# A gated mix of a long convolution and a token-mixing MLP: row-wise first layer norm, x1 seeded into PSUM for the fourth product, mirrored frequency sets, and a new written-out order

## Chip, cores and metric

The kernel runs on one core of one Trainium2 chip. The metric is device time in microseconds (us). In the text PE is TensorE (PEld its weight loads), ACT is ScalarE, DVE is VectorE, POOL is GpSimd and SP is SyncE, which here only issues DMAs.

## What is computed

The input q (called x here) has 2048 tokens of 640 channels in bfloat16. The reference, cut to what matters:

```python
x = A_q
g = sigmoid((x * gate_w).sum(-1, keepdims=True))
# branch a: shift convolution over 4 taps, times v, then a causal convolution of length 2048 per channel
kv = shift_conv(k, shift_k) * v
a  = x * (irfft(rfft(pad(kv)) * rfft(pad(ssm_k)))[:2048] + kv * ssm_D)
# branch b: two MLP halves; the first shifts four channel groups by +1, -1, +2, -2 tokens
h  = gelu(layernorm(x) @ w1)
x1 = x + shift_groups(h) @ w2
b  = x1 + gelu(layernorm(x1) @ w3) @ w4
out = g * a + (1 - g) * b
```

## The kernel before

**Tiling.** A token is numbered 1024c + 8p + rho: p is the partition, and the 16 pairs (rho, c) are the token tiles, 128 tokens by 640 channels each. A "row" is one rho, so two tiles. Everything lies in one SBUF tensor (`arena`) and one PSUM tensor (`PS`), and the trace shows only these two names. PSUM is dealt out as four pairs of banks: each matmul job takes a pair, and gives it back when its evictions are done.

**Branch b.** LN1 takes mean and variance of x with `bn_stats` on DVE (L640, tag `bn`), the power -0.5 on POOL (L646, `ln`), and writes the normalised tile on ACT (L465, `xn`). PE transposes it (L620, `xTp`) and ACT evicts the transposes (L480, `xTe`). `mm1` (L715) multiplies by w1, with a gelu on eviction (`gelu1`). One fifth of each product, the tail (`gelu1t`), is moved between partitions by DMAs on POOL's queue (L743, `tail`). `mm2` (L760) multiplies by w2, ten matmuls of 320 columns per tile, and two matmuls with the identity (L762) add x. Its eviction makes x1 (`x1`). LN2 takes its sums on ACT for half of the rows (with an accumulator in the `x1` eviction, and a `Square` pass, `sq`) and with `bn_stats` on DVE for the other half. `xn` is again on ACT, and a DMA transpose (L615, `xT`) writes the operand of `mm3` (L792, gelu on eviction `gelu3`). `mm4` (L808) has 24 matmuls per tile and two more with the identity for x1 (L810). Its eviction `B` scales by 1 - g and overwrites x1 in place. w3 is loaded over w1 and w2, so its DMA (POOL's queue) waits for the last `mm2`.

**Branch a.** `kv` on DVE (L453, the line of every `tensor_tensor`) makes k_shift * v in four chunks of 128x2560, eight instructions each. The filter is transposed on PE (L578, `tap`) and evicted by ACT (L583). The convolution is a transform over 512 odd frequencies, for each of two halves of the channels (half 0, 1) and each of two frequency sets (kap 0, 1). That is four *units*, numbered 2*half + kap. `forward` (L844, `fwdh` for the filter, `fwdk` for kv) has 8 jobs of four 320-column matmuls per signal and unit, each evicted by ACT (L480, 128x640: `Sh`, `Sk`). On DVE a unit then runs `bh`, `win`, `bk` (butterflies and window), `pw` (the complex product) and `fold`, one after the other, on slots of 128x5120. `inverse` (L934, `inv`) has 8 rows of eight matmuls per half. ACT evicts them with the gate g (`gy`, 128x320), DVE multiplies by q and adds to the tile that `B` left (`fin`), and SP writes the output.

**What sets the order.** Nothing is ordered by hand in the body. `Prog.schedule` simulates all engines with assumed costs and lets ready instructions go by a table of ranks per tag and stage (`P.PRIO`). What comes out is a fixed list per engine, and each engine runs its list strictly in order. `assign_waits` puts a semaphore wait ahead of an instruction where another engine's result is needed.

In before, the fixed lists have these places that the prediction speaks of: PE runs 40 of the 256 `fwd` matmuls ahead of `mm2`, 88 between the `mm2` jobs and 36 behind the last of them; the rest comes between `mm3`, `mm4` and `inv`. DVE's 15 instructions from 54.53 us on are the last twelve of `kv` with three of `bh` of unit 0 among them; the last of `kv` is the last of the 15. The two 128x1280 instructions after DVE's 1.74 us wait for ACT, at 82.85 us, are `win` of unit 0, and its last `fold` (unit 3) ends the run of 102 instructions from 126.85 us on.

Of the kernel before, what the change touches and what calls it, by code (L numbers as in the profile page):

```python
# [1 line left out]

# [15 lines left out]
class Job:  # L18
    __slots__ = ("pair", "pe", "evicts")

    def __init__(self):
        self.pair = None
        self.pe = None
        self.evicts = []


class Node:
    __slots__ = ("idx", "eng", "fns", "deps", "users", "cost", "lat", "bytes", "kind", "job", "prio",
                 "start", "end", "base", "ordinal", "seq", "waits", "inc", "value", "sem", "final", "snap", "missing", "tag")

    def __init__(self, idx, eng, fns, cost, kind, tag):
# [8 lines left out]
        self.lat = 0.1  # L40
        self.bytes = 0
        self.job = None
        self.prio = 0.0
# [9 lines left out]
        self.missing = 0  # L53

# [24 lines left out]
class Prog:  # L79
    def __init__(self, nc):  # L80
        self.nc = nc
        self.nodes = []
        self.stage = ""
        self.writers = {}
        self.readers = {}
# [28 lines left out]

    def op(self, eng, fn, r=(), w=(), cost=0.2, job=None, group=None, tag=""):
        node = self._new(eng, [fn], cost, "c", r, w, group, tag)
        if job is not None:
            node.deps.add(job.pe)
            node.job = job
            job.evicts.append(node)  # L120
        return node

    def pe(self, fns, r=(), cols=0, tag=""):
        job = Job()
        cost = cols / 2400.0 + 0.004 * len(fns) + 0.02
        node = self._new("pe", fns, cost, "c", r, (), None, tag)
        node.job = job
        job.pe = node
        return job

    def dma(self, queue, fn, r=(), w=(), nbytes=0, cost=0.1, kind="dma", group=None, final=False, tag=""):
        node = self._new(queue, [fn], cost, kind, r, w, group, tag)
        node.bytes = nbytes
        node.final = final
        return node

    RATE = 390e3
    PRIO = {}

    def schedule(self):  # L140

        for n in self.nodes:
            n.base = frozenset(n.deps)
            for d in n.deps:
                d.users.append(n)
        for n in reversed(self.nodes):
            tail = max((u.prio for u in n.users), default=0.0)
            n.prio = tail + (n.cost if n.kind == "c" else n.cost + 2.0 + n.bytes / self.RATE)
        for n in self.nodes:
            n.prio = self.PRIO.get(n.tag, n.prio)  # L150
        self._forward()

    def _forward(self):
        nodes = self.nodes
        rate = self.RATE
        for n in nodes:
# [3 lines left out]
            if n.job is not None:  # L160
                n.job.pair = None
# [4 lines left out]
        pair_job = [None] * PAIRS  # L166
        link = 0.0
        xlink = 0.0

        def arrive(n):  # L170
            known_at[n] = max((d.end + (d.lat if d.eng != n.eng else 0.06) for d in n.deps), default=0.0)
            ready[n.eng].append(n)

        def open_pairs():
            return [(pair_free[i], i) for i in range(PAIRS)
                    if pair_job[i] is None or all(v.end is not None for v in pair_job[i].evicts)]
# [7 lines left out]
        while left:  # L184
            best = None
            pairs = open_pairs()
            for e in ENGS:
                if e == "pe" and not pairs:
                    continue
                for n in ready[e]:  # L190
                    t = max(known_at[n], free[e])
                    if e == "pe":
                        others = [d.end for ev in n.job.evicts for d in ev.deps if d is not n]
                        if any(x is None for x in others):
                            continue
                        t = max(t, min(pairs)[0], max(others, default=0.0) - n.cost)
# [12 lines left out]
            elif n.kind == "dma":  # L209
                link = max(link, t) + n.bytes / rate  # L210
                n.end = link + 2.0
            else:
                xlink = max(xlink, t + 1.0) + 1.2
                n.end = xlink + 1.5
            if e == "pe":
                pick = min(pairs)[1]
# [803 lines left out]
```

## Time and profile before

| what | value |
|---|---|
| runs of before | 254.81, 255.53 and 256.13 us (median 255.53) |
| span of the profiled execution, first to last instruction | 253.7 us |
| median less that span | 1.8 us |
| mean granted TensorE clock | 0.990 |
| DMA over the span | 27.81 MB, of which 20.55 MB on the hardware queue that SP issues to |
| DVE `tensor_tensor` (L453), all forms | 195.8 us busy in 208 instructions |

The profiled execution's own time is its span and a little around it. No separate figure is listed for it, so 1.8 us, the median less the span, stands for what lies around. A row of a timeline reads: start, duration, engine, line, operation, output and input, count, and in brackets the idle time ahead of it with what ended it. The chain of work that ended last is read back from the last instruction. In it "PE PS L808 x12" means that PE itself was the limit there, and "DMA arena<-in_B_w_dram" that a load was. Instructions overlap at their ends. So a run of n equal instructions divided by n is the time that each costs its engine, which is less than the mean duration of one.

### The profile page before, as it was taken

The page shows a single profiled execution, that of the slowest core. Times are in us where ns is not written, and L with a number is a line of the kernel's source. Part 1 is how long each engine was busy: PE and PEld are TensorE (multiplying, and loading weights), DVE is VectorE, ACT ScalarE, POOL GpSimd, SP SyncE. Part 2 cuts the span into 40 slices and gives each one's busy share as a digit, 9 for nine tenths or more (in the row PEclk, how much of TensorE's full clock was granted, in tenths as well). Part 3 has the DMA queues.
Part 4 walks back from the last instruction along what each step waited for, and adds up shares of the span by engine and source line. Part 5 has one row for each costly group of instructions (what it writes and reads, how often), then busy time and mean ns, then how long its engine had stood idle before and what let it go on. Part 6 is the DMA issues. An engine that isn't in the chain of part 4 may idle for free.

```text
span 253.7 us, 3951 instructions
## 1 busy us (share of the span) xinstructions
PE 227.5 (90%) x1585; PEld 144.7 (57%) x1585; DVE 221.8 (87%) x323; ACT 166.9 (66%) x244; POOL 31.2 (12%) x43
## 2 busy tenths in 40 slices
PE   3037799999999999989999999999999999899992
PEld 1033446956677777634675476677545774377771
DVE  3959999999997999999299999999999999919084
ACT  6085899988699979954888867721744214417283
POOL 6114513006132030202100000000000000000000
PEclk9999999799999999999999999999999999999998
DMA  7999996001057003630056600000000000194034
GB/s 226 225 377 412 411 372 260 3 0 30 16 186 292 0 3 78 199 141 0 0 54 129 126 3 4 0 3 0 0 0 3 0 0 3 21 386 138 27 103 155
DMA packets 21666, 27.81 MB, mean 110 GB/s; under 512 B 12001, under 2 KB 17377, under 8 KB 21393
## 3 DMA queue, kind: packets, MB, share of 16 engines
q1 hardware_dynamic: 19520, 20.55, 25.6%
q0 software_dynamic: 1840, 5.71, 7.1%
q10 hardware_dynamic: 288, 1.31, 1.7%
q8 instruction: 12, 0.20, 0.3%
q14 instruction: 6, 0.04, 0.1%
HBM read 21.79 MB, written 2.62 MB: 96 GB/s over the span
## 4 chain that ended last, share of the span: by engine, by line
PE 80%; DMA 8%; ACT 8%; SPq 2%; issue 1%; DVE 0%; ACTq 0%
PE PS L808 21%; PE PS L792 20%; PE PS L844 12%; PE PS L760 9%; DMA arena<-in_B_w_dram 8%; PE PS L934 7%; PE PS L715 5%; ACT arena L480 5%; ACT arena L465 3%; SPq L487 2%; PE PS L578 2%; PE PS L762 2%; PE PS L810 2%; PE PS L673 1%; DVE arena L453 0%
## 5 line engine op out<-in xcount | busy, mean ns | idle before, releaser
L453 DVE TENSOR_TENSOR arena<-arena 128x1280 bf16<-128x1280 bf16 (+2 forms) x208 | 195.8, 999 | 19.9 <-ACT arena L480 12.8
L480 ACT ACTIVATE arena<-PS 128x640 bf16<-128x640 f32 (+3 forms) x129 | 96.4, 828 | 35.4 <-PE PS L792 24.2
L808 PE MATMUL PS<-arena 128*128 128x320 bf16 x384 | 56.7, 299 | 1.1 <-ACT arena L480 1.1
L792 PE MATMUL PS<-arena 128*128 128x512 bf16 x240 | 52.8, 379 | 1.8 <-DMA arena<-in_B_w_dram 1.8
L480 ACT ACTIVATE arena<-PS,arena 128x320 bf16<-128x320 f32 (+1 forms) x48 | 27.8, 613 | 39.2 <-PE PS L810 36.5
L808 PEld LDWEIGHTS PS<-arena 128*128 128x128 bf16 x384 | 37.4, 98 | 16.6 <-ACT arena L480 1.6
L792 PEld LDWEIGHTS PS<-arena 128*128 128x128 bf16 x240 | 23.4, 98 | 29.4 <-issue 2.1
L465 ACT ACTIVATE arena<-arena 128x640 bf16<-128x640 bf16 (+2 forms) x42 | 33.9, 853 | 6.6 <-DVE arena L647 5.8
L844 PE MATMUL PS<-arena 128*128 128x320 bf16 x256 | 36.2, 299 | 0.0
L844 PEld LDWEIGHTS PS<-arena 128*128 128x128 bf16 x256 | 25.0, 98 | 10.4
L715 PE MATMUL PS<-arena 128*128 128x512 bf16 x100 | 24.3, 396 | 5.7 <-DMA arena<-in_B_w_dram 3.2
L760 PE MATMUL PS<-arena 128*128 128x320 bf16 x160 | 26.2, 299 | 0.1
L640 DVE BATCH_NORM_STATS2 arena<-arena 128x6 f32<-128x320 bf16 x48 | 20.6, 471 | 3.2 <-DMA arena<-in_A_q_dram 3.1
L715 PEld LDWEIGHTS PS<-arena 128*128 128x128 bf16 x100 | 9.7, 101 | 17.7 <-DMA arena<-in_B_w_dram 3.5
L760 PEld LDWEIGHTS PS<-arena 128*128 128x128 bf16 x160 | 15.6, 98 | 6.3 <-issue 0.4
L934 PE MATMUL PS<-arena 128*128 128x320 bf16 x128 | 17.9, 299 | 0.0
L934 PEld LDWEIGHTS PS<-arena 128*128 128x128 bf16 x128 | 12.5, 98 | 5.0
L646 POOL TENSOR_TENSOR arena<-arena 128x4 f32<-128x4 f32 x6 | 9.4, 1566 | 32.3 <-DVE arena L645 32.3
L743 POOL DMA_DIRECT2D arena<-arena x18 | 9.5, 536 | 27.7 <-ACT arena L480 27.7
L620 PE MATMUL PS<-arena 128*128 128x128 bf16 x80 | 6.6, 242 | 4.5 <-ACT arena L465 4.5
L810 PE MATMUL PS<-arena 128*128 128x320 bf16 x32 | 9.6, 299 | 0.0
L762 PE MATMUL PS<-arena 128*128 128x320 bf16 x32 | 9.6, 299 | 0.0
(46 smaller groups left out, 71.3 us busy)
## 6 DMA issues: line engine op xcount, KB each, us to landing
arena<-in_A_q_dram SPq DMA_DIRECT2D x6, 640.0 KB, 7.1
arena<-in_B_w_dram POOLq DMA_DIRECT2D x4, 960.0 KB, 7.0
arena<-in_A_k_dram SPq DMA_DIRECT2D x4, 640.0 KB, 14.5
arena<-in_A_v_dram SPq DMA_DIRECT2D x4, 640.0 KB, 15.1
arena<-in_A_ssm_k_dram SPq DMA_DIRECT2D x5, 512.0 KB, 18.9
out_dram<-arena SPq DMA_DIRECT2D x16, 160.0 KB, 2.0
arena<-in_A_q_dram ACTq DMA_DIRECT2D x2, 640.0 KB, 5.6
arena<-cF SPq DMA_DIRECT2D x1, 1024.0 KB, 20.9
```

The source lines that it names most:

```text
L453: return dve(lambda e: e.tensor_tensor(o, a, b, op), [a, b], [o], n, tag=tag, **kw)
L465: node = P.op("act", lambda e, ps: e.activation(o, i, func, **kw), r=r, w=[o], cost=c_act(n, naps, acc is not None), tag=tag, group=group)
L480: node = P.op("act", lambda e, ps: e.activation(ov, inner(ps), func, **kw), r=r, w=[o], cost=c_act(n, len(r), acc is not None), job=job, t ...
L640: dve(lambda e, o=o, x=x: e.bn_stats(o, x), [x], [o], 640, tag="bn", group=("bn", g, i))
L715: fns.append(lambda e, ps, b=b, c=c, lhsT=lhsT, sc=sc: e.matmul(bank(ps, b, 512), lhsT, XT[:, c, 2 * sc:2 * sc + 2, :], start=(c == 0), st ...
L760: fns.append(lambda e, ps, hh=hh, ft=ft, lhsT=lhsT: e.matmul(bank(ps, hh, 320), lhsT, w2v[:, ft, 320 * hh:320 * hh + 320], start=(ft == 0) ...
L762: fns.append(lambda e, ps, hh=hh, c=c, rho=rho: e.matmul(bank(ps, hh, 320), ident, X[:, c, rho, 320 * hh:320 * hh + 320], start=False, sto ...
L792: fns.append(lambda e, ps, b=b, ft=ft, c=c, sc=sc: e.matmul(bank(ps, b, 512), w3v[:, c, 128 * ft:128 * ft + 128], XT[:, c, 2 * sc:2 * sc + ...
L808: fns.append(lambda e, ps, hh=hh, ft=ft, lhsT=lhsT: e.matmul(bank(ps, hh, 320), lhsT, w4v[:, ft, 320 * hh:320 * hh + 320], start=(ft == 0) ...
L810: fns.append(lambda e, ps, hh=hh, c=c, rho=rho: e.matmul(bank(ps, hh, 320), ident, X[:, c, rho, 320 * hh:320 * hh + 320], start=False, sto ...
L844: fns.append(lambda e, ps, r=r, ri=ri, s=s, b=b, rhs=rhs: e.matmul(bank(ps, b, 320), FM[:, kap, r, s, ri, :], rhs, start=(s == 0), stop=(s ...
L934: fns.append(lambda e, ps, kap=kap, ri=ri, c=c, r=r, s=s, n=n: e.matmul(bank(ps, c, 320), GM[:, kap, ri, r, s, :], Qs[kap][:, r, ri, c, :] ...
```

## The change

It is a rewrite of the body and of the scheduler's assumptions, in these parts.

1. **LN1 by rows.** x comes in eight loads of 128x1280 (rows 2sc and 2sc+1 of one c) ahead of everything else. Groups for LN1 are row 0, row 1, then pairs. `xn` of LN1 and of LN2 is a `tensor_scalar` on DVE, (x - mean) * rs, in place of an ACT activation. `mm1` of rows 0 and 1 goes by single rows. All LN2 sums come from ACT (`LN2_DVE = ()`), so no `bn_stats` is left there.
2. **x1 seeded.** For `mm4`, ACT copies x1 into the PSUM pair ahead of the job (`seed4`, 16 copies of 128x640), and all 24 matmuls accumulate onto it. The 32 identity matmuls of `mm4` are gone. `mm2` keeps its own (now first in the job).
3. **Mirrored sets share PSUM.** The second frequency set is taken in the order 255 - 2j. For even r its transform is that of the first set plus one table term, so the job of set 0 is evicted, two more matmuls add to the same pair, and it is evicted again for set 1. Per signal and half that makes 56 matmuls in place of 64, with the same 16 evictions. `forward` now does both sets in one go.
4. **Products over their operand.** `pw` is ten 128x2560 instructions, partly in place, in place of six of 128x2560 and eight of 128x1280. `kv` has three 128x5120 and two 128x2560 per chunk in place of eight 128x2560. `fold` has two 128x2560 and four 128x1280 in place of eight 128x1280 (unit 2 keeps the old form). q is loaded per half into freed slots.
5. **New ranks** and new assumed costs in the scheduler, hence a new list for every engine. 40 small matmuls run on PE before the first data (`warm`).

```diff
+LN1_GROUPS = ((0,), (1,), (2, 3), (4, 5), (6, 7))
+LN2_DVE = ()
+SEED4 = (0, 1, 2, 3, 4, 5, 6, 7)
-                act(b, X[:, c, rho, :], ACTF.Identity, 640, scale=stat(l, 5)[:, g, i:i + 1],
-                    bias=stat(l, 6)[:, g, i:i + 1], tag="xn")
+        ts(b, X[:, c, rho, :], mean, rs[:, rho, c:c + 1], ALU.subtract, ALU.mult, 640, tag="xn")
...
+    def seed(job, c, rho, tag, on, fns, rd):
+        if not on:
+            rd.append(X[:, c, rho, :])
+            for hh in range(2):
+                fns.append(lambda e, ps, hh=hh: e.matmul(
+                    bank(ps, hh, 320), ident, X[:, c, rho, 320 * hh:320 * hh + 320], start=True, stop=False))
+            return
+        x = X[:, c, rho, :].rearrange("p (h d) -> p h d", h=2)
+        P.seed(job, lambda e, ps: e.activation(two(ps, 320), x, ACTF.Copy), [X[:, c, rho, :]], c_act(640, psum=False), tag)
...
-                        bank(ps, hh, 320), lhsT, w4v[:, ft, 320 * hh:320 * hh + 320], start=(ft == 0), stop=False))
-                fns.append(lambda e, ps, hh=hh, c=c, rho=rho: e.matmul(
-                    bank(ps, hh, 320), ident, X[:, c, rho, 320 * hh:320 * hh + 320], start=False, stop=True))
+                        bank(ps, hh, 320), lhsT, w4v[:, ft, 320 * hh:320 * hh + 320], start=False, stop=(ft == 11),
+                        skip_group_check=rho in SEED4))
...
+        for r in (0, 2, 1, 3):
             for ri in range(2):
+                job = go(None, lambda s: FM0[:, r, s, ri, :], r, ri, (0, 1), S0[:, r, ri], True, sig)
+                if r % 2 == 0:
+                    go(job, lambda s: FM2[:, r // 2, ri, :], r, ri, (MIRROR[r // 2][ri],),
+                       S1_[:, r, ri if r == 0 else 1 - ri], False, sig)
+                else:
+                    go(None, lambda s: FM1[:, r // 2, s, ri, :], r, ri, (0, 1), S1_[:, r, ri], True, sig)
...
+        tt(im(R0), kb[0], hb(1, 1), ALU.mult, 2560, tag="pw")
+        tt(im(T1), kb[1], hb(1, 0), ALU.mult, 2560, tag="pw")
+            tt(T1, T1, R0, ALU.add, 2560, tag="pw")
+        tt(im(R1), kb[0], hb(0, 1), ALU.mult, 2560, tag="pw")
+        tt(kb[1], kb[1], hb(0, 0), ALU.mult, 2560, tag="pw")
+            tt(kf[1], kf[1], R1n, ALU.add, 2560, tag="pw")
+        tt(im(T0), kb[0], hb(1, 0), ALU.mult, 2560, tag="pw")
+        tt(kb[0], kb[0], hb(0, 0), ALU.mult, 2560, tag="pw")
+        tt(K[:, 0], K[:, 0], Tb[:, 1], ALU.subtract, 2560, tag="pwz")
+        tt(K[:, 1], K[:, 1], Tb[:, 0], ALU.add, 2560, tag="pwz")
```

**The changed lists**, as the built program has them. PE: 40 small matmuls; LN1 transposes and `mm1`; the gate; four `tap` jobs (c = 1 tokens of the filter), four `mm2` jobs, four `tap`, four `mm2`; then 92 `fwd` matmuls (56 of `fwdh`, 36 of `fwdk`) and eight `mm2` jobs with two `fwd` matmuls among them; then 42 `fwd` with `mm3` starting after them. 88 `fwd` are left for later. The `tap` evictions wait for the last two instructions of `kv` chunk 1 on DVE, whose scratch lies where the filter is written (before, it lay elsewhere). The first `mm2` waits for the first `tap` eviction and for two tail DMAs of the last `mm1` stage. `win` of unit 0 waits for the 25th of the `fwd` evictions. SP's list is: x (with w1 in between), the halo of c = 1, shift_k, v and k of c = 0, the transform table, the rest of the halo, v, ssm_k, gate_w, the remaining k and v, w2. The loads of q now stand behind the transposes and wait for the last `fwdk`. POOL's list keeps the w3 load behind the last `mm2`.

## Prediction before the run

> **What bounds the kernel now.** I read the page's busy times and slices first, then the chain that ended last in order of time, then the busy time of each engine by stretches, then groups and timelines.
>
> ```profile
> PE 227.5 (90%) x1585; PEld 144.7 (57%) x1585; DVE 221.8 (87%) x323; ACT 166.9 (66%) x244; POOL 31.2 (12%) x43
> PE   3037799999999999989999999999999999899992
> DVE  3959999999997999999299999999999999919084
> ACT  6085899988699979954888867721744214417283
> ```
>
> Two engines are near the span of 253.7 us: PE is full from the eighth slice on, DVE from the fourth to the 34th. ACT is full only in the first half.
>
> ```profile
> 6.30 14.21 DMA arena<-in_B_w_dram
> 20.55 6.94 PE PS L715 x25
> ...
> 47.77 4.37 PE PS L578 x50
> ...
> 64.10 0.84 PE PS L760 x5
> ...
> 102.60 6.13 DMA arena<-in_B_w_dram
> 108.73 0.27 issue
> 109.00 13.11 PE PS L792 x60
> ...
> 220.24 1.03 ACT arena L480
> ...
> 239.96 8.71 PE PS L934 x64
> ...
> 250.26 0.49 DVE arena L453
> ```
>
> The chain gives four landmarks: PE starts `mm1` at 20.55 (w1 has landed), `mm2` at 64.10, `mm3` at 109.00 (w3 has landed), and its last matmul ends at 248.67. The rest, 5.0 us, is eviction, `fin` and output.
>
> ```profile
> 64.10:109.00 44.90, 43.09 (x316) 30.87 (x317) 42.70 (x61) 40.00 (x76) 7.93 (x8) 1.00 0.38 118
> 109.00:248.70 139.70, 138.54 (x876) 85.33 (x876) 120.71 (x159) 75.66 (x109) 2.58 (x2) 1.00 0.19 51
> ```
>
> Columns: stretch, length, busy PE, PEld, DVE, ACT, POOL, clock, DMA. From `mm3` on PE idles 1.2 of 139.7 us, ACT 64. So in the last stretch a matmul saved is time saved, as long as DVE keeps up; in the stretch before it PE, DVE and ACT are all within 5 us of full, and what counts there is which of them the new order waits for.
>
> **The last stretch (from `mm3` on), by PE.** From the chain: 64 matmuls of 320 columns take 8.71 us, 0.136 each.
>
> - The 32 identity matmuls of `mm4` go: 32 x 0.136 = -4.35 us.
> - `fwd` left for this stretch: 256 - 40 - 88 - 36 = 92 before, 88 after: -0.54.
> - `mm3`, the other `mm4` matmuls and `inv` are unchanged.
> - The 16 seeds come onto ACT.
>
> ```profile
> L480 ACT ACTIVATE arena<-PS 128x640 bf16<-128x640 f32 x84 | 52.5, 733 | 4.3 <-PE PS L762 4.0 <-PE PS L548 0.2
> L465 ACT ACTIVATE arena<-arena 128x640 bf16<-128x640 bf16 x40 | 33.5, 885 | 6.6 <-DVE arena L647 5.8 <-DMA arena<-arena 0.6
> ```
>
> No row writes PSUM from ACT. The nearest, PSUM to SBUF and SBUF to SBUF at the same size, are 0.73 and 0.89 us; each instruction costs its engine 52.5/84 = 0.63 to 33.5/40 = 0.84. I take 0.8, or 13 us in all, against 64 us of ACT idle: hidden. Uncovered it is priced among the rivals. In the changed list each seed stands one or two gelus ahead of its job. What is queued behind a waiting seed on ACT is the next `B` or gelu, and the pair it holds is one of four, so I leave the 1.0 us stall at 220.24 in as an allowance for such seams and drop nothing else. Stretch after: 139.7 - 4.9 = 134.8 us.
>
> ScalarE: Activation LUTs in the Trainium skill, section "Step-by-step: what each stage is for", says that ACT writes PSUM faster than SBUF. By it a seed would cost less than 0.8 us; the sum stays, since the seeds are hidden either way.
>
> **DVE in the last stretch.** It must not come later than PE.
>
> ```profile
> L453 DVE TENSOR_TENSOR arena<-arena 128x2560 bf16<-128x2560 bf16 x72 | 103.9, 1485 | 0.4
> L453 DVE TENSOR_TENSOR arena<-arena 128x1280 bf16<-128x1280 bf16 x104 | 78.9, 819 | 5.9 <-ACT arena L480 5.6
> L640 DVE BATCH_NORM_STATS2 arena<-arena 128x6 f32<-128x320 bf16 x48 | 20.6, 471 | 3.2 <-DMA arena<-in_A_q_dram 3.1
> L642 DVE BATCH_NORM_AGGREGATE arena<-arena 128x2 f32<-128x12 f32 x24 | 4.6, 198 | 0.2
> L645 DVE TENSOR_SCALAR arena<-arena 128x4 f32<-128x4 f32 x6 | 1.0, 164 | 0.0
> L453 DVE TENSOR_TENSOR arena<-arena 128x640 bf16<-128x640 bf16 x32 | 14.9, 490 | 13.6 <-ACT arena L480 7.2 <-DMA arena<-in_A_q_dram 5.5
> 82.85 1.56 DVE L453 TENSOR_TENSOR arena<-arena 128x1280 bf16<-128x1280 bf16 x2 [1.74 <-ACT arena L480]
> 126.85 95.38 DVE L453 TENSOR_TENSOR arena<-arena 128x1280 bf16<-128x1280 bf16 x102 [3.85 <-ACT arena L480]
> ```
>
> The last two rows: `win` of unit 0 starts at 82.85, the last `fold` ends at 222.23, 139.4 us with some 5 us idle. By its group a 2560 costs 1.44 and a 1280 0.76. Per unit, `pw` goes from 6 x 1.44 + 8 x 0.76 = 14.7 to 10 x 1.44 = 14.4, and `fold` from 8 x 0.76 = 6.1 to 2 x 1.44 + 4 x 0.76 = 5.9 in three units: -1.8 over four. `bn_stats` of LN2 leaves DVE; ten of its 16, with five aggregates, stood after 82.85: -(10 x 0.43 + 5 x 0.19) = -5.3. In come 12 `xn`, and five rows of `fin`, ten 640s at 0.47 = 4.7. An `xn` is a 640-wide `tensor_scalar`, which no row shows: above the 4-wide one (0.16) and, reading one tensor for two, I take it not above the `tensor_tensor` of its width (0.49); at one element per step as in `bn_stats` it would be 2 x 0.43 = 0.86, the far end. I take 0.33, the middle of the near two: 12 x 0.33 = 4.0. Sum: -1.8 - 5.3 + 4.0 + 4.7 = +1.6. So the last `fold` comes 141 us behind `win` of unit 0.
>
> VectorE: DVE Perf Modes, section "The perf-mode tier table", gives bf16 `tensor_scalar` four elements per cycle where `tensor_tensor` has two. An estimate from that page's cycle table would be 0.23 us per `xn`. By it DVE would have 32 x 0.1 = 3 us less to do; no run here shows it yet.
>
> **The first two stretches.** x in small loads and ahead of w2 and k lets LN1 start, and w1 stands fourth on SP, so PE's 20.55 falls to perhaps 13. I count nothing of that as gain, because the next landmark hangs on DVE:
>
> ```profile
> 5.31 0.89 DVE L640 BATCH_NORM_STATS2 arena<-arena 128x6 f32<-128x320 bf16 x2
> ...
> 16.69 0.89 DVE L640 BATCH_NORM_STATS2 arena<-arena 128x6 f32<-128x320 bf16 x2 [2.88 <-DMA arena<-in_A_q_dram]
> ...
> 26.24 4.28 DVE L453 TENSOR_TENSOR arena<-arena 128x2560 bf16<-128x2560 bf16 x3
> ...
> 54.53 20.77 DVE L453 TENSOR_TENSOR arena<-arena 128x2560 bf16<-128x2560 bf16 x15
> ```
>
> `tap` evictions wait for the end of `kv` chunk 1. DVE starts at about 5.0; the LN1 statistics take 16.4 (from 5.31 to 26.2 without one `kv` and 3.1 of waiting), the 16 `xn` 5.3, waits for loads 1, small things 0.5, and chunks 0 and 1 each 3 x 2.8 + 2 x 1.44 = 11.3. (A 5120 is two 2560s less one fixed cost, which is 2 x 0.76 - 1.44 = 0.08.) Together 50.8, less the last product 1.4: first `tap` eviction at 49.4. All of `kv` ends near 74.5 (75.3 before), ahead of its use near 76. From 49.4 ACT is the bound:
>
> ```profile
> 45.38 5.92 ACT L583 ACTIVATE arena<-PS 128x1280 bf16<-128x1280 bf16 x5
> 70.82 0.70 ACT L480 ACTIVATE arena<-PS 128x640 bf16<-128x640 f32 x1
> 71.42 0.19 ACT L480 ACTIVATION_READ_ACCUMULATOR arena<-PS 128x1 f32 x1
> 71.65 0.74 ACT L465 ACTIVATE arena<-arena 128x640 bf16<-128x640 bf16 x1
> 83.32 9.06 ACT L480 ACTIVATE arena<-PS 128x640 bf16<-128x640 f32 x15 [0.50 <-PE PS L762]
> ```
>
> Its list holds 8 `tap` (1.18 each, 9.4), 8 `x1` and 4 `sq` (0.82 each, start to start with the accumulator read, 9.8) and 25 `fwd` evictions (9.06/15 = 0.60, 15.1): 34.3 us. PE's share of the same, 80 `tap` (4.37/50 each), 8 `mm2` jobs and 92 `fwd`, is 7 + 13 + 12.5 = 32.5, so the shared PSUM pairs, which save PE matmuls but no eviction, gain nothing here. `win` of unit 0 starts at 49.4 + 34.3 = 83.7, 0.8 later than before.
>
> ```profile
> L620 PE MATMUL PS<-arena 128*128 128x128 bf16 x80 | 6.6, 242 | 4.5 <-ACT arena L465 4.5
> L480 ACT ACTIVATE arena<-PS 128x512 bf16<-128x512 f32 x4 | 2.4, 601 | 0.8 <-PE PS L715 0.7
> L743 POOL DMA_DIRECT2D arena<-arena x18 | 9.5, 536 | 27.7 <-ACT arena L480 27.7
> arena<-arena POOLq DMA_DIRECT2D x12, 32.0 KB, 3.9
> GB/s 226 225 377 412 411 372 260 3 0 30 16 186 292 0 3 78 199 141 0 0 54 129 126 3 4 0 3 0 0 0 3 0 0 3 21 386 138 27 103 155
> ```
>
> Two covers to watch. The first `mm2` also waits for two tail DMAs of the last `mm1`, 3.9 us each to land: that `mm1` follows the last `xn` (36.6) by 0.8 for ten transposes and 7.6 for 35 matmuls (13.11/60 each, from the chain), and after the gelu (0.6) and four issues (0.54 each) the tail lands at 52, by when ACT still has `tap` evictions to do until 54. And `kv` chunk 1 needs its k, with 11.9 MB ahead of or in its load: by the slices of 6.34 us that is 35.5 us, its use 39.
>
> From there eight `mm2` jobs at 1.63 (twelve matmuls x 0.136) start about 0.6 sooner, at 83.1, with one pair of `fwd` (0.3) and 1.2 of lag to ACT, which has `x1` and `sq` (1.64) for each: the last ends at 97.6, against 102.3. The w3 load starts then; the chain shows 0.3 + 6.13 + 0.27 = 6.7 to the first `mm3`: 104.3, against 109.0, **-4.7 us**. It comes from the 36 `fwd` behind `mm2` having become 42 and 96 `fwd` rather than 128 having gone before. The cover of the load is 42 x 0.136 = 5.7 us of PE, or 11 evictions = 6.6 of ACT.
>
> **Sum.** `mm3` at 104.3, plus 134.8 = 239.1, plus the tail 5.0 = 244.1 span, plus 1.8 around it: **246 us**. DVE's last `fold` is at 83.7 + 141 = 224.7; PE then has the last ten `inv` rows (10.9) and a `mm4` job (3.3) to go, 238.9: the two agree to a microsecond, so either can be the one that is late.
>
> **Rivals.**
>
> *Both stretches shorten (239).* If the early lists hang on PE and not on DVE's chunk 1, the first stretches shrink by PE's start, 20.55 to 13, less 1. For it: ACT's 34.3 and PE's 32.5 are close, and an `xn` shorter than 0.33 brings chunk 1 sooner. Against: the ten instructions of chunks 0 and 1 stand between. 246 - 6.5 = 239.5, at best 238. Chance 0.18.
>
> *`xn` at one element per step (254.5).* At 0.86 the 16 LN1 `xn` delay chunk 1 by 8.5 us, and everything behind it: 246 + 8.5, no change that could be told. Chance 0.08.
>
> *The seeds are not hidden (260, slower).* A seed can only start when an earlier job's eviction has freed a pair, and it holds one of four until its `mm4` ends. If each stands in PE's way for its length, 16 x 0.89 = 14.2 us. It makes the kernel slower from (256.8 - 246)/16 = 0.68 us per seed on. For it: ACT's list is in order, and a seed late behind a gelu leaves PE waiting with nothing else in its own list. Against: ACT idles 64 of 139.7 us there. Chance 0.05.
>
> *The change doesn't do what it says (251).* If the matmuls saved only lengthen PE's waits for DVE, the last stretch stays 139.7: 246 + 4.9. Chance 0.06.
>
> **How the numbers follow.** The forecast (241 to 250) has 0.63, the rivals what is given. The range 238 to 253 leaves out the third rival, most of the second and a little of the first. A measurement here tells about 0.5%, 1.3 us, from no change. Faster by more than that holds the forecast, the first, the last and a quarter of the second: 0.89; within it 0.05; slower 0.06.
>
> **What would show it.** Right: the first `mm3` near 104, just behind the w3 load; the last matmul 135 us later, with no identity matmul in `mm4`; `win` of unit 0 near 84; ACT above 95% from 49 to 84; seeds that PE hardly waits for. Wrong: `mm3` outside 99 to 109, PE idle over 4 us behind seeds, `xn` beyond 0.5 us, or `kv` waiting for k.

## The result, and the profile after

| | before | after |
|---|---|---|
| runs, median (range) | 255.32 us (254.81 to 256.13, 4 runs) | 244.55 us (244.37 to 244.66, 4 runs) |
| ratio after / before, 95% interval | | 0.9556 [0.9519, 0.9593] |
| span of the profiled execution | 253.7 | 242.4 |
| first `mm3` | 109.00 | 103.18 |
| last matmul ends | 248.67 | 237.33 |

The change takes 10.8 us off (4.4% by the ratio). The forecast was 246.0 us, with a range from 238 to 253. Of the profiled 11.3 us, 5.8 come ahead of `mm3` and 5.55 behind it.

The page of after, busy times and slices:

```profile
PE 224.5 (93%) x1574; PEld 142.3 (59%) x1586; DVE 221.8 (92%) x290; ACT 157.4 (65%) x255; POOL 32.8 (14%) x38
PE   7279989999999999699999999999999999999991
DVE  3998889999999899989999989789999999999484
ACT  2066685489999998968744668752554951564583
```

DVE has the same 221.8 us of work as before in a shorter span; it is now as full as PE, 92 and 93%. ACT still has room in the second half, where the seeds are.

Busy time by stretches of after (columns as before: stretch, length, PE, PEld, DVE, ACT, POOL, clock, DMA share, GB/s):

```profile
49.40:83.10 33.70, 32.67 (x266) 21.74 (x264) 32.89 (x33) 32.84 (x59) 5.66 (x8) 1.00 0.40 100
103.18:237.33 134.15, 133.49 (x832) 81.10 (x838) 124.67 (x148) 80.16 (x124) 6.61 (x3) 1.00 0.21 48
```

In the first row, from 49.40 (where the first `tap` eviction was forecast; it came at 50.06) to `win` of unit 0, PE, DVE and ACT are all at 97 to 98%, so this row alone cannot say which of them is the bound. In the last stretch PE idles 0.7 of 134.15 us (some of that are matmul records missing from the trace: 832 where other runs of the same list show 840).

The chain of after, with the landmarks:

```profile
24.06 3.54 POOL arena L750
...
29.37 3.53 POOL arena L750
...
50.06 4.62 ACT arena L735 x4
...
95.45 4.09 ACT arena L621 x8
99.64 3.16 ACT arena L621 x5
103.18 2.10 PE PS L965 x9
...
226.45 10.88 PE PS L1137 x80
```

Two things are new here. POOL's power (`ln`, L750) is on the path twice, 3.5 us each. And ahead of `mm3` the chain as the profile follows it goes through ACT's evictions, not through the w3 load; experiment 8 shows that PE waited for the load all the same. Groups of after by shape (busy, mean ns of one, idle before):

```profile
L590 DVE TENSOR_TENSOR arena<-arena 128x5120 bf16<-128x5120 bf16 x12 | 33.7, 2821 | 0.1
L750 POOL TENSOR_TENSOR arena<-arena 128x4 f32<-128x4 f32 x7 | 16.0, 2286 | 31.1 <-DVE arena L590 26.3 <-DVE arena L595 4.8
L595 DVE TENSOR_SCALAR arena<-arena 128x640 bf16<-128x640 bf16 x32 | 12.4, 437 | 4.3 <-POOL arena L750 3.3 <-DMA arena<-arena 0.9
L607 ACT ACTIVATE arena<-arena 128x640 bf16<-128x640 bf16 x16 | 12.0, 753 | 0.2
L909 ACT ACTIVATE PS<-arena 128x640 f32<-128x640 bf16 x16 | 11.0, 734 | 0.1
```

An `xn` costs 12.4/32 = 0.39 us, a seed 11.0/16 = 0.69, and a `kv` product of 5120 2.81. DVE's list up to `win` of unit 0:

```profile
16.91 0.45 DVE L595 TENSOR_SCALAR arena<-arena 128x640 bf16<-128x640 bf16 x1 [0.55 <-POOL arena L750]
...
19.48 0.49 DVE L756 BATCH_NORM_STATS2 arena<-arena 128x6 f32<-128x320 bf16 x1 [0.88 <-DVE arena L758]
...
23.88 2.82 DVE L590 TENSOR_TENSOR arena<-arena 128x5120 bf16<-128x5120 bf16 x1
...
27.70 1.60 DVE L595 TENSOR_SCALAR arena<-arena 128x640 bf16<-128x640 bf16 x5 [0.88 <-POOL arena L750]
...
32.92 0.80 DVE L595 TENSOR_SCALAR arena<-arena 128x640 bf16<-128x640 bf16 x2 [0.91 <-POOL arena L750]
...
83.10 7.55 DVE L590 TENSOR_TENSOR arena<-arena 128x1280 bf16<-128x1280 bf16 x8 [0.59 <-ACT arena L621]
```

Four waits, 3.2 us together, stand ahead of the first `tap` eviction at 50.06: three for POOL and one (19.48) that the profile puts down to DVE itself. In the list two memsets stand there that wait for the last of the four-matmul sets of L691 on PE:

```profile
15.50 1.29 PE L691 MATMUL PS<-arena 1*128 1x320 bf16 x4
16.90 1.25 PE L822 MATMUL PS<-arena 128*128 128x256 bf16 x5
18.08 1.29 PE L691 MATMUL PS<-arena 1*128 1x320 bf16 x4
```

That set ends at 19.37, because a single-row `mm1` of 1.25 us stands between the two halves. That the 0.88 us are a wait for it is read from the list; experiment 6 bears it out.

### The profile page after: what moved, and what is told of

The parts are those of the page before. It is cut to its first block, busy times and chain, and to the rows that moved or that the text cites. A ratio compares the mean times of both kernels' runs of the same rounds, so it can differ in the third digit from the quotient of the medians.

```text
span 242.4 us, 3935 instructions
## 1 busy us (share of the span) xinstructions
PE 224.5 (93%) x1574; PEld 142.3 (59%) x1586; DVE 221.8 (92%) x290; ACT 157.4 (65%) x255; POOL 32.8 (14%) x38
## 4 chain that ended last, share of the span: by engine, by line
PE 66%; ACT 16%; DVE 11%; POOL 3%; DMA 2%; issue 1%; ACTq 0%; DVEq 0%
PE PS L983 22%; PE PS L965 21%; ACT arena L621 11%; PE PS L1137 7%; DVE arena L590 7%; PE PS L1014 6%; PE PS L926 4%; ACT arena L735 4%; POOL arena L750 3%; PE PS L822 2%; DVE arena L595 2%; DMA arena<-in_A_q_dram 2%; DVE arena L756 2%; PE PS L788 1%; ACT arena L607 1%
## 5 line engine op out<-in xcount | busy, mean ns | idle before, releaser
L590 DVE TENSOR_TENSOR arena<-arena 128x2560 bf16<-128x2560 bf16 (+4 forms) x184 | 194.3, 1110 | 8.6 <-ACT arena L621 6.6
L965 PE MATMUL PS<-arena 128*128 128x512 bf16 x232 | 51.7, 379 | 2.5 <-ACT arena L621 2.0
L983 PE MATMUL PS<-arena 128*128 128x320 bf16 x384 | 53.5, 299 | 0.0
L983 PEld LDWEIGHTS PS<-arena 128*128 128x128 bf16 x384 | 37.5, 98 | 15.2 <-ACT PS L909 0.2
L965 PEld LDWEIGHTS PS<-arena 128*128 128x128 bf16 x240 | 23.3, 98 | 29.4 <-issue 2.4
L1014 PE MATMUL PS<-arena 128*128 128x320 bf16 x224 | 34.2, 300 | 0.7 <-ACT arena L621 0.5
L1014 PEld LDWEIGHTS PS<-arena 128*128 128x128 bf16 x224 | 19.5, 97 | 14.4 <-ACT arena L621 6.6
L822 PE MATMUL PS<-arena 128*128 128x512 bf16 (+1 forms) x121 | 24.7, 361 | 1.8 <-ACT arena L621 1.4
L926 PE MATMUL PS<-arena 128*128 128x320 bf16 x160 | 24.3, 299 | 0.0
L750 POOL TENSOR_TENSOR arena<-arena 128x4 f32<-128x4 f32 (+1 forms) x9 | 17.5, 1949 | 37.5 <-DVE arena L590 26.3
L822 PEld LDWEIGHTS PS<-arena 128*128 128x128 bf16 x125 | 12.8, 106 | 11.5 <-issue 1.7
L926 PEld LDWEIGHTS PS<-arena 128*128 128x128 bf16 x160 | 15.7, 98 | 6.1
L595 DVE TENSOR_SCALAR arena<-arena 128x640 bf16<-128x640 bf16 (+3 forms) x47 | 14.7, 355 | 4.3 <-POOL arena L750 3.3
L1137 PE MATMUL PS<-arena 128*128 128x320 bf16 x128 | 18.0, 299 | 0.0
L756 DVE BATCH_NORM_STATS2 arena<-arena 128x6 f32<-128x320 bf16 x32 | 13.4, 463 | 3.6 <-DMA arena<-in_A_q_dram 2.7
L1137 PEld LDWEIGHTS PS<-arena 128*128 128x128 bf16 x128 | 12.5, 98 | 5.2 <-issue 0.3
L607 ACT ACTIVATE arena<-arena 128x640 bf16<-128x640 bf16 (+2 forms) x18 | 12.4, 694 | 0.2
L909 ACT ACTIVATE PS<-arena 128x640 f32<-128x640 bf16 x16 | 11.0, 734 | 0.1
## 6 DMA issues: line engine op xcount, KB each, us to landing
arena<-in_A_k_dram SPq DMA_DIRECT2D x4, 640.0 KB, 11.3
```

What stands on the lines that cost most here:

```text
L590: return dve(lambda e: e.tensor_tensor(o, a, b, op), [a, b], [o], c_tt(n), tag=tag, **kw)
L595: return dve(lambda e: e.tensor_scalar(o, a, s1, s2, op0=op0, **kw2), [a] + sc, [o], c_ts(n), tag=tag, **kw)
L607: node = P.op("act", lambda e, ps: e.activation(o, i, func, **kw), r=r, w=[o], cost=c_act(n, naps, acc is not None, psum=False), tag=tag, ...
L750: P.op("pool", lambda e, ps: e.tensor_tensor(r, v, hv, ALU.pow), r=[v, HALF], w=[r], cost=1.1, tag="ln")
L756: dve(lambda e, o=o, x=x: e.bn_stats(o, x), [x], [o], 0.393, tag="bn", group=("bn", id(mv), rho, c))
L822: fns.append(lambda e, ps, b=b, c=c, lhsT=lhsT: e.matmul(bank(ps, b, 256 * n), lhsT, XT[:, c, r0:r0 + n, :], start=(c == 0), stop=(c == 4)))
```

## Experiments

Theory A is the prediction's account: up to the first `tap` eviction DVE's list sets the time, up to the last `mm2` ACT does, from `mm3` on PE, with DVE close behind. The rivals are named in the expectations. All times are to be set against 244.55 (after) and its ratio. In experiments 1 to 5, 7 and 8 the lists of all engines are those of after, with the extra instructions put in behind the planning. In the others the lists were planned anew: in 6 and 12 they differ from after only ahead of the first `tap`, in 9 from the start of `mm3` on (besides the `xn` that move), in 10 and 11 throughout.

**1. The identity matmuls back.**

```diff
+        # ahead of the 24 matmuls of a job; the seed writes one column per bank
+        e.matmul(bank(ps, hh, 320), ident, X[:, c, rho, 320 * hh:320 * hh + 320], start=True, stop=False)   # hh = 0, 1
-        e.activation(two(ps, 320), x, ACTF.Copy)
+        e.activation(two(ps, 320)[:, :, 0:1], x[:, :, 0:1], ACTF.Copy)
```

> The changed kernel with the 32 identity matmuls of mm4 back on PE, two ahead of each job, and every list otherwise as it was; the seed copies shrink to one column per bank, so ACT keeps its instruction but hardly any of its work. Theory A (the last stretch is PE's: it idles 0.8 us of 134): 32 x 0.136 = 4.35 us come back, 244.5 + 4.4 = 248.9, all of it between the first mm3 and the last matmul. Rival B (DVE's folds set the end, so matmuls there lengthen or shorten only PE's waits): 244.5 to 245.5.

Measured: 248.10 us (247.96 to 248.36), ratio 0.9715 [0.9688, 0.9742], 3.55 us more than after. Its last stretch and the start of `mm3`:

```profile
102.41:241.05 138.64, 138.54 (x872) 84.42 (x872) 125.43 (x148) 72.99 (x125) 6.61 (x3) 1.00 0.21 48
```
```profile
102.41 2.32 PE L969 MATMUL PS<-arena 128*128 128x512 bf16 x10 [1.29 <-DMA arena<-in_B_w_dram]
```

PE is busy 138.54 of 138.64 us with 872 matmuls, where the runs with 840 records have 134.25 to 134.7: the 32 cost 3.9 to 4.3 us. B is out. The run also shows something of `mm3`: PE waits there for the load of w3, and starts 0.8 us sooner than in after with the same ACT list ahead of it.

**2. A longer seed.**

```diff
+        e.activation(pair(ps)[:, :, 320:512], x[:, :, 0:192], ACTF.Copy)    # unused columns of the same pair
         e.activation(two(ps, 320), x, ACTF.Copy)
```

> The changed kernel with a second copy behind each of the 16 seeds, 384 elements wide, into columns of the same PSUM pair that nothing reads. Same lists otherwise. By the 0.69 us of a 640-wide seed it should cost ACT some 0.45 to 0.5 each, 7 to 8 us in all. Theory A (the seeds are hidden in ACT's idle time): 244.5, at most 1 us more. Rival C (a seed stands in PE's way for part of its length, so PE's seams grow with it): up to 244.5 + 7.5 = 252.

In the kernel that ran, the second copy stands ahead of the seed, not behind it. Measured: 244.88 us (244.53 to 245.37), ratio 0.9586 [0.9552, 0.9621]: 0.3 us more, within what can be told. ACT's busy time went from 157.4 to 163.7 us, 0.39 per copy. C would have shown 6.3 us. Seeds are hidden, with room.

**3. Mirrored matmuls twice.**

```diff
             job = P.pe(fns, ...)                       # forward
+            if not first: fns[0:0] = list(fns)         # 4 matmuls for a mirrored set, as before the change
```

> The changed kernel with the two matmuls of each mirrored set issued twice into the same PSUM pair, so that a signal and half has 64 matmuls again, as before; evictions and lists stay. It adds the mirrored term twice, so the second set's values are wrong. 16 of the 32 more matmuls stand ahead of mm3, where ACT was the bound by the prediction, and 16 behind its start. Theory A: the early 16 cost nothing (0 to 0.5), the late 16 cost 16 x 0.136 = 2.2, so 246.7 (246.5 to 247.2). Rival D (PE is the bound in both places): 4.35, 248.9. Rival B (DVE sets the end): 244.5.

Measured: 244.88 us (244.62 to 245.13), ratio 0.9588 [0.9561, 0.9614]: 0.3 us more, where A said 2.2 and D 4.4.

The issue of the w3 load on POOL, in after and here, and the last stretch here:

```profile
95.71 1.75 POOL L633 DMA_DIRECT2D arena<-in_B_w_dram  x2 [20.35 <-PE PS L1014]
```
```profile
95.91 1.75 POOL L634 DMA_DIRECT2D arena<-in_B_w_dram  x2 [20.59 <-PE PS L927]
```
```profile
101.83:237.80 135.97, 135.94 (x856) 83.26 (x856) 125.91 (x151) 82.21 (x127) 6.61 (x3) 1.00 0.20 51
```

The early 16 were free, as A said: the w3 load, which waits for the last `mm2`, is issued at 95.91 and not at 95.71. The late 16 are in the last stretch: 135.97 against 134.15, 1.8 us. But `mm3` began at 101.83 and not at 103.18, which took 1.35 us back. So the miss is not in the matmuls: the time from the w3 issue to the first `mm3` was 5.9 us here and 7.5 in after (more on this in experiment 8).

**4. More work for DVE ahead of the first tap.**

```diff
+            e.bn_stats(scratch, X[:, c, rho, 0:320])   # ahead of each xn of LN1
             e.tensor_scalar(b, X[:, c, rho, :], mean, rs, op0=subtract, op1=mult)
```

> The changed kernel with one more bn_stats of 320 elements (0.43 us) on DVE ahead of each of the 16 xn of LN1, its result unused; lists otherwise the same. Theory A (the first tap eviction and all behind it hang on DVE's list up to kv chunk 1): 16 x 0.43 = 6.9 us more work, of which at most the 3.3 us that DVE waits for POOL there can swallow a part: first tap eviction from 50.1 to 53.7 to 57, and the time 248 to 251.4. Rival E (the early lists hang on PE's start, on ACT or on loads): 244.5 to 245.5.

Measured: 248.62 us (248.18 to 248.9), ratio 0.9732 [0.9703, 0.9761], 4.1 more than after.

```profile
55.02 4.62 ACT L736 ACTIVATE arena<-PS 128x1280 bf16<-128x1280 bf16 x4 [0.67 <-DVE arena L591]
```
```profile
107.73 2.32 PE L970 MATMUL PS<-arena 128*128 128x512 bf16 x10 [1.70 <-ACT arena L622]
```

The first `tap` eviction comes 5.0 us later (55.02), `mm3` 4.55, the end 4.1. Of the 6.9 us added, 1.9 fell into DVE's waits. E is out: a delay in DVE's list ahead of the first `tap` reaches the end, most of it undiminished.

**5. More work for DVE behind it.** The same `bn_stats` ahead of each `xn` of LN2.

> The changed kernel with one more bn_stats of 320 elements (0.43 us) on DVE ahead of each of the 16 xn of LN2, its result unused; lists otherwise the same. Four stand ahead of win of unit 0 (1.7 us, of which 0.6 falls into a wait for ACT), twelve behind it (5.2 us): DVE is given 6.3 us. In the changed kernel's profile the last fold ends near 223.8 and the last matmul 13.5 us later, where ten inv rows alone need 10.9, so DVE has some 2.6 us to spare, and it waits 2 to 3 us for ACT on its way. Theory A (PE sets the end, DVE is 2 to 3 us behind being late): 244.5 + 1 to 3.7, I take 246.7. Rival B (DVE is the one that is late, or exactly tied): 244.5 + 6.3 = 250.8. Rival F (DVE has slack throughout): 244.5 to 245.

Measured: 245.87 us (245.77 to 246.03), ratio 0.9630 [0.9597, 0.9662]: 1.3 more, inside A's bounds (1 to 3.7) and below the 2.2 that A took.

```profile
138.39 1.31 PE L1019 MATMUL PS<-arena 128*128 128x320 bf16 x8 [1.54 <-ACT arena L622]
223.63 1.25 PE L1142 MATMUL PS<-arena 128*128 128x320 bf16 x8 [0.18 <-DVE arena L591]
```

PE has new waits, 1.54 and 0.18 us, the second for DVE's `fold`. So DVE is a few us from being late, not tied.

**6. LN1 in pairs of rows again.**

```diff
-LN1_GROUPS = ((0,), (1,), (2, 3), (4, 5), (6, 7))
+LN1_GROUPS = ((0, 1), (2, 3), (4, 5), (6, 7))
-SPLIT = (0,)        # mm1 of rows 0 and 1 by single rows
+SPLIT = ()
```

> The changed kernel with LN1's groups in pairs of rows, as before the change (rows 0 and 1 together, and the first mm1 by pairs too); the lists move only up to the first tap. PE's first transposes and mm1 come some 4 us later than 10.64 and 13.28. Theory A (the next landmark hangs on DVE's list, which has the same instructions up to kv chunk 1): first tap eviction at 50 within 1 us, 244.5 within 0.7. Rival E (PE's earlier start is worth its length): 4 us more, 248.5.

Measured: 241.92 us (241.82 to 242.0), ratio 0.9474 [0.9447, 0.9501]: **2.6 us less than after** (by the ratios 0.9%, and the two intervals do not touch). Neither theory said so.

```profile
13.38 2.29 PE L788 MATMUL PS<-arena 128*128 128x128 bf16 x20 [8.47 <-DVE arena L595]
...
100.08 2.32 PE L965 MATMUL PS<-arena 128*128 128x512 bf16 x10 [0.43 <-ACT arena L621]
219.71 1.25 PE L1137 MATMUL PS<-arena 128*128 128x320 bf16 x8 [0.30 <-DVE arena L590]
```
```profile
22.58 2.82 DVE L590 TENSOR_TENSOR arena<-arena 128x5120 bf16<-128x5120 bf16 x1
...
26.40 1.59 DVE L595 TENSOR_SCALAR arena<-arena 128x640 bf16<-128x640 bf16 x5 [0.88 <-POOL arena L750]
...
31.63 0.80 DVE L595 TENSOR_SCALAR arena<-arena 128x640 bf16<-128x640 bf16 x2 [0.91 <-POOL arena L750]
...
81.57 7.56 DVE L590 TENSOR_TENSOR arena<-arena 128x1280 bf16<-128x1280 bf16 x8 [0.34 <-ACT arena L621]
```

PE starts its transposes 2.7 us later (13.38) and nothing comes of it, as A said. But DVE's first `kv` begins at 22.58 and not at 23.88: the waits at 16.91 (0.55) and 19.48 (0.88) are gone, the two at 26.40 and 31.63 are as they were. The first `tap` eviction follows at 48.77 (1.3 sooner), `win` of unit 0 at 81.57 (1.5 sooner), the w3 issue at 94.18 (1.5 sooner). From there `mm3` took 5.9 us and not 7.5, and its 100.08 is 3.1 sooner. In the last stretch (135.0 us) 0.85 us are lost again, and PE now waits for a `fold` (219.71). So going by rows cost 1.3 us on DVE, which became 1.5 at the w3 issue. The other 1.6 us at `mm3` are the time in which w3 landed, and nothing shows that the rows lengthened it (experiment 8).

**7. `kv` in smaller pieces.**

```diff
-e.tensor_tensor(t, src, sb, op)                        # 128x5120
+e.tensor_tensor(t[:, j], src[j], sb[:, j], op)         # 128x2560, j = 0, 1
```

> The changed kernel with each 128x5120 instruction of kv issued as two of 128x2560; lists otherwise the same. Cost on DVE by the groups: 12 x 0.08 = 1.0 us, half of it ahead of the first tap eviction. POOL's two powers that run beside kv take 3.54 and 3.53 us there and 0.77 where no kv runs, and DVE waits 0.9 us for each. Theory G (POOL's instruction is held while one DVE product runs, so it lasts as long as that product): they shorten by up to 1.4 us, DVE's two waits all but go, first tap eviction at 50.06 + 0.5 - 1.8 = 48.8 and the time 243.5 to 244.5. Rival H (the power is slow by itself whatever DVE does): they stay at 3.5, and the time is 245 to 245.5.

Measured: 243.74 us (243.51 to 244.21), ratio 0.9547 [0.9519, 0.9576], 0.8 less than after by the medians, which the ratio does not bear out (its interval and that of after overlap almost wholly).

```profile
24.21 2.20 POOL L756 TENSOR_TENSOR arena<-arena 128x4 f32<-128x4 f32 x1 [3.01 <-DVE arena L595]
28.58 3.59 POOL L756 TENSOR_TENSOR arena<-arena 128x4 f32<-128x4 f32 x1 [2.16 <-DVE arena L595]
```

One of the two powers shortened, from 3.53 to 2.20 us, and DVE's wait for it went; the other stayed at 3.59. The first `tap` eviction came at 49.62, 0.4 sooner. G holds in half: POOL got in between two products once, and once it did not.

**8. A small first piece of w3.**

```diff
-for a, b in ((0, 768), (768, 1536)):
+for a, b in ((0, 256), (256, 1536)):
     load("pool", w3v[:, :, a:b], ...)
```

> The changed kernel with w3's two loads cut at column 256 instead of 768, so that the first job of mm3 needs only the first, small one (0.33 MB of 1.97); PE, ACT and DVE lists unchanged. In the changed kernel PE stands 2.0 us ahead of mm3, which the page puts down to ACT's evictions; but with the same evictions (ended 102.7) mm3 began at 102.41 in the run with the identity matmuls back and at 101.83 in the run with the mirrored matmuls doubled, so I doubt it. Theory A (the first half of w3 is what PE waits for): mm3 starts at 101.3 to 101.6, the time falls by 1.5 to 1.9 less what DVE, 2 to 3 us from late, takes back: 242.8 to 243.4. Rival I (ACT's evictions hold the PSUM pair that mm3 needs): mm3 at 103, 244.5.

Measured: 244.53 us (243.87 to 245.01), ratio 0.9571 [0.9543, 0.9599]: no change.

```profile
101.70 2.32 PE L965 MATMUL PS<-arena 128*128 128x512 bf16 x10 [0.50 <-ACT arena L621]
105.59 15.28 PE L965 MATMUL PS<-arena 128*128 128x512 bf16 x70 [0.49 <-DMA arena<-in_B_w_dram]
```

`mm3` did begin 1.5 us sooner (101.70) with the same evictions ahead of it, so the 2.0 us of after were a wait for w3's first half, and the releaser that the page names (ACT) is not the one. That rules I out. But 0.49 us come back at 105.59, where PE waits for the second piece, and the last matmul ends 0.6 us sooner than in after. The rest is not in the time, and the 242.8 to 243.4 us that A gave did not come.

Why the load lands later in some traces can be read from its first half, which lands in sixteen parts. In after fifteen of them are in by 5.6 us behind the issue and the last at 7.0; with LN1 in pairs (experiment 6) all are in by 5.7. In after a packet of the instruction queue (`q8` on the page, 0.02 MB) begins 1.7 us behind the issue and takes 1.8 us. Seven traces with w3 in two halves (after and experiments 1, 2, 4, 5, 7 and 9) have such a packet 1.6 to 2.5 us behind the issue: their last part lands at 6.3 to 7.0 us and `mm3` begins 6.8 to 7.5 us behind the issue. Five (experiments 3, 6, 10, 11 and 12) have none there: 5.7 to 5.9 us, and 5.9 to 6.2. So the late part goes with that packet in all twelve, but no edit moved the packet alone.

**9. `xn` of LN2 back on ACT.**

```diff
-ts(b, X[:, c, rho, :], mean, rs, ALU.subtract, ALU.mult, 640, tag="xn")              # LN2 only
+act(b, X[:, c, rho, :], ACTF.Identity, 640, scale=rs, bias=mean, tag="xn")
```

> The changed kernel with the 16 xn of LN2 on ACT again, as an activation with scale and offset per token (the offset is the mean itself here, so the normalised values are wrong); the lists of PE, and of DVE and ACT but for these 16, have the same order. ACT gets four of them ahead of win of unit 0 and twelve behind it, at 0.84 each in the kernel before; DVE loses 16 x 0.38 = 6.1 us. Theory A (up to the last mm2 ACT is the bound, so xn on DVE is what brought mm3 forward; behind it ACT has room and PE sets the end): win of unit 0 later by 4 x 0.84 = 3.4 us, near 86.5, mm3 later by 3.4 to 6.7 (up to eight xn ahead of it), the last stretch not shorter: 248 to 251. Rival B (DVE is the bound everywhere, its relief of 6.1 us pays): 244.5 or less.

Measured: 261.36 us (259.95 to 261.53), ratio 1.0219 [1.0183, 1.0255]: 16.8 more than after and some 2% more than before. The direction is A's; the size is far beyond the 3.5 to 6.5 us that it gave. One premise of the expectation does not hold: the lists were planned anew, and from the start of `mm3` on PE and ACT have another order (two of the `mm3` jobs moved behind the first two of `mm4`). PE, DVE, ACT and POOL around the two places:

```profile
78.94 8.79 PE L1017 MATMUL PS<-arena 128*128 128x320 bf16 x44 [3.89 <-ACT arena L621]
...
108.22 2.10 PE L968 MATMUL PS<-arena 128*128 128x512 bf16 x9 [1.36 <-ACT arena L621]
...
123.55 2.33 PE L968 MATMUL PS<-arena 128*128 128x512 bf16 x10 [3.50 <-ACT arena L621]
132.37 8.20 PE L986 MATMUL PS<-arena 128*128 128x320 bf16 x48 [6.49 <-ACT PS L912]
```
```profile
88.78 7.56 DVE L590 TENSOR_TENSOR arena<-arena 128x1280 bf16<-128x1280 bf16 x8 [3.92 <-ACT arena L621]
...
107.74 12.98 DVE L590 TENSOR_TENSOR arena<-arena 128x2560 bf16<-128x2560 bf16 x13
```
```profile
110.79 10.84 POOL L750 TENSOR_TENSOR arena<-arena 128x4 f32<-128x4 f32 x1 [7.64 <-DVE arena L590]
```
```profile
121.66 0.92 ACT L607 ACTIVATE arena<-arena 128x640 bf16<-128x640 bf16 x1 [8.37 <-POOL arena L750]
...
131.51 2.59 ACT L912 ACTIVATE PS<-arena 128x640 f32<-128x640 bf16 x4
```

The first place is A's: four `xn` on ACT (3.35 us in its trace) bring `win` of unit 0 to 88.78, 5.7 us later, and `mm3` to 108.22, 5.0 later. That is more than the `xn` themselves: ACT also waits 0.6 us for POOL's power ahead of them and 1.2 us behind them for PE, which had stood for 3.9 us and had a granted clock of 0.69 from 78.94 to 87.70. So work for ACT between 50 and 83 delays `win`, where 16 matmuls more on PE moved the w3 issue by 0.2 us (experiment 3). The second is new. POOL's power for the next `xn` starts at 110.79 and takes **10.84 us**, until DVE's run of thirteen instructions (107.74 to 120.7), products all but one, is over; ACT waits 8.37 us for it at the head of its list, with gelus of `mm3` behind it and four seeds behind them, and PE waits 3.50 and 6.49 us. How much of the 16.8 us another order would avoid was not tested. In after the `xn` stands on DVE itself: DVE stops for the power, 1.0 us, and so lets it through.

**10. Other ranks, on top of the pairs.**

```diff
-return 0.07 + n / 1920.0      # assumed cost of a product; likewise xn, activations, power, DMA rate, landing of x
+return 0.08 + n / 1882.0
-PRIO = {"xn:1": 182, "xn:0": 181, ...}
+PRIO = {...}                  # all ranks anew
```

> The run with LN1 in pairs of rows, and with other ranks for every list, found with assumed costs that are set to what the profiles show (xn 0.38, a power 2.2, products 0.08 us more, x landing 1.7 us later). No instruction is added or taken away. Theory A (the early lists lose 2 to 4 us to seams between DVE, ACT and PE, which another order can close; PE's last stretch of 134 to 135 us can't shrink): mm3 at 98 to 100, time 239.5 to 241.5, against 241.9 for the pairs alone. Rival (the order was already at the engines' bounds): 241.9 or more.

Measured: 244.54 us (243.94 to 244.71), ratio 0.9568 [0.9538, 0.9598]: 2.6 more than the pairs alone. The rival holds.

```profile
25.21 1.52 DVE L596 TENSOR_SCALAR arena<-arena 128x640 bf16<-128x640 bf16 x4 [3.50 <-PE PS L789]
```

With the new order DVE waits 3.5 us for PE to give back an `xn` buffer, ahead of its first `kv`. The first `tap` eviction is at 50.55 and not at 48.77.

**11. The same with four `xn` of LN1 on ACT.**

```diff
+XN1_ACT = {(r, 1) for r in range(4, 8)}
+act(b, X[:, c, rho, :], ACTF.Identity, 640, scale=rs, bias=-mean * rs, tag="xn")
```

> As the run with other ranks, and with four of the 16 xn of LN1 (rows 4 to 7, c = 1) on ACT, which had 10 us and more of idle time ahead of the first tap; DVE loses 4 x 0.38 = 1.5 us there, less 0.3 for two small products that make the offset. Theory A (all up to the last mm2 hangs on DVE's list ahead of the first tap): 1.2 us less than the run with other ranks, 238.5 to 240.5. Rival (these xn stand behind gelus on ACT, so that PE and then DVE wait for them): the same as that run or more.

Measured: 242.30 us (241.96 to 243.05), ratio 0.9491 [0.9464, 0.9519]. 2.2 less than the run before it, where A said 1.2, but outside the 238.5 to 240.5 that it gave, and no better than the pairs in the old order. The ranks differ too, so what the four `xn` did by themselves stays open.

**12. Pairs and `kv` in halves together.**

> The two edits that helped together: LN1 in pairs of rows and each 128x5120 instruction of kv as two of 128x2560. Theory A (both act on DVE's list ahead of the first tap, and add): 241.9 less 0.4 to 0.8, 241.1 to 241.5, with one of the two waits of 0.9 us for POOL gone. Rival (what kv in halves saved was the same seam that the pairs already closed): 241.9 to 242.3.

Measured: 241.60 us (241.3 to 241.74), ratio 0.9427 [0.9404, 0.9450]: faster than before and after, and 0.3 less than the pairs alone, which is at the edge of what can be told (0.5% by the ratios: before took 256.27 us beside these runs, 255.22 beside those of experiment 6). It lies between A (241.1 to 241.5) and its rival (241.9 to 242.3). One of the two powers took 1.04 us, and DVE's wait for it is gone. The first `tap` eviction came at 48.34 (48.77 with the pairs alone), `mm3` at 100.16.

```profile
100.16:234.82 134.66, 134.41 (x840) 81.10 (x840) 125.94 (x151) 81.73 (x126) 6.61 (x3) 1.00 0.23 52
```

In the last stretch PE idles 0.25 of 134.66 us.

## Why the prediction was right

**The last stretch (134.8 forecast, 134.15 in the profile).** Right, and by its terms: the identity matmuls were worth 3.6 us in time and 3.9 to 4.3 of PE (forecast 4.35), the late mirrored ones 1.8 us. The stall of 1.0 us that was kept as an allowance did not come: PE idles 0.7 us in all. So a price that was too high and a stall that was missing offset each other in part.

**The seeds.** Right that they are hidden; the price was too high, 0.69 us instead of 0.8. The section "Step-by-step: what each stage is for" in the Trainium skill's ScalarE: Activation LUTs says that ACT writes PSUM faster than SBUF; the trace hardly tells. A seed into PSUM lasts 0.73 us and a `sq` of the same size into SBUF 0.75, and the two do different work.

**DVE in the last stretch.** The last `fold` ended at 223.8 (forecast 224.7). An `xn` costs 0.39 us, above the 0.33 that was taken, inside the bounds. The 0.23 us that was estimated from the cycle table of the Trainium skill's VectorE: DVE Perf Modes (section "The TRN2 errata — SBUF-src ops pay a fixed extra latency per instruction") is not met, and one lasts 0.44 us; the measurement decides. That either of PE and DVE could be the late one was too close: DVE was given 6.3 us in experiment 5 and 1.3 came out.

**The first stretches.** The first `tap` eviction was forecast at 49.4 and came at 50.06, `win` of unit 0 at 83.7 and 83.10, `mm3` at 104.3 and 103.18. That DVE's list sets the first of them is shown by experiment 4, and experiments 3 and 9 bear out that ACT is the bound behind it: the shared PSUM pairs gain nothing there, and `xn` on ACT costs more than its length. Three steps were off:

- *"I count nothing of that as gain"* (PE's earlier start). There is indeed none, but by rows is not free. The prediction allowed 1 us of waits on DVE and there are 3.2. Two of them, 1.4 us, exist only by rows. With pairs the kernel takes 2.6 us less, of which they explain 1.3 to 1.5; the rest goes with w3 landing sooner.
- The last `mm2` ended some 2 us sooner than the 97.6 forecast: its eight jobs began at 81.93, ahead of `win`, where 83.1 was forecast, and ran at the 1.63 us each that was taken. The 1.2 us of lag to ACT that the sum had was not there: the w3 load was issued at 95.71, 0.3 us behind the last of these matmuls.
- *"6.7 to the first `mm3`"* for the w3 load. It took 7.5 us from its issue in after, and 5.9 to 7.5 over the runs with the same order from the first `tap` on. The longer ones go with an instruction packet during the load (experiment 8). This miss and the one before it have opposite signs, so `mm3` came closer to its forecast than its terms did, which is luck.

The 96 `fwd` that the prediction has ahead of the last `mm2` are 94 by its own list; nothing is worked out from them.

**Where the 10.8 us come from.** Behind `mm3`, 5.55: 3.6 to 4.3 for the identity matmuls, 0.5 for four matmuls of `forward` fewer, the rest seams. Ahead of it, 5.8: with `xn` of LN2 on ACT again 5.0 of them are gone, the shared PSUM pairs gave nothing, and LN1 by rows took some 1.5 away. What the products over their operand, the loads of x and the new ranks gave was not tested by itself. Single undoings can't be added up: `xn` of LN2 back on ACT costs 16.8 us, more than the whole change. Some 12 us of that fall behind the start of `mm3`, where the power is held up, in lists that before does not have. So it is not a gain over before.

**The rivals.** *Both stretches shorten* did not come with PE's early start. *One element per step* is out (0.39 us). *The change doesn't do what it says* is out (experiment 1). *Seeds not hidden* is out as the change stands, but experiment 9 shows its mechanism: when ACT is held up by 8 us, the gelus and four seeds behind it come late and PE waits 6.5 us.

## What to carry to other kernels

Ask of every step that is made finer which waits it puts into the engine that is the bound: an earlier start on PE was worth nothing, and the two waits that it put into DVE's list cost 1.3 us there and 1.5 at the next landmark. Taking work off an engine that is nearly full (ACT, by `xn` on DVE) pays in the stretch where that engine is the bound, and a matmul saved pays in full only where PE is. Where the profile names a releaser for a wait on several things, move one of them alone before believing it.

## What the runs showed of the hardware

A small instruction on POOL (a power of 128x4) takes 1.0 us beside `bn_stats`, 3.5 us when a DVE product of 5120 elements begins just ahead of it, and 10.84 us beside the rest of the run in experiment 9. In every trace a power that met a DVE product ended about 0.9 us behind the end of a product. In this direction the traces agree with the Trainium skill, SBUF — State Buffer, section "SBUF: two separate sides": a DVE instruction with two SBUF inputs and one of GpSimd that reads SBUF exclude each other for the whole instruction. No run here shows the other direction: in after, products that ran while a power ended took 1.48 us as ever.

Which product a power has to wait for varied. In after two powers, one behind the other, got in during a run of products that had no gap:

```profile
123.50 14.38 DVE L590 TENSOR_TENSOR arena<-arena 128x1280 bf16<-128x1280 bf16 x14
126.67 3.66 POOL L750 TENSOR_TENSOR arena<-arena 128x4 f32<-128x4 f32 x2 [18.62 <-DVE arena L590]
```

In the same trace the one at 105.10 let the end of one product pass and took 2.94 us; in experiment 7 one got in and one did not; in experiment 9 the power let nine ends pass. What decides this is not shown. So on this kernel a power is sure to be short only where DVE itself stops for it.
